# Cosine attention and a gated feed-forward layer: from 112-row tiles in pairs of heads to 128-lane tiles in quads, with every engine's order written by hand

## The chip, the cores and the metric

One core of one Trainium2 chip runs the kernel. The metric is the device time of one execution in microseconds (us), the median over the runs of a kernel. The profile is of one execution; its times are us unless marked ns.

## What is computed

```python
q_n = q / (norm(q, axis=-1) + 1e-06)          # q, k, v: 8 batches, 12 heads, 448 rows, 64 columns, fp32
k_n = k / (norm(k, axis=-1) + 1e-06)
attn = softmax(q_n @ k_n.T / tau)             # tau = 0.1
x = (attn @ v) with the heads side by side    # 3584 x 768
H = max(x @ w_h, 0);  T = sigmoid(x @ w_t + b_t)   # w_h, w_t: 768 x 768
out = T * H + (1 - T) * x                     # 3584 x 768, fp32
```

Both kernels write T as (1 + tanh)/2, so the softmax's denominator carries a factor 2 (the column of 2.0 beside v) and the bias a factor 0.5. Scores are at most 1/tau, so no maximum is subtracted.

## The kernel before

All 448 rows of a head are four chunks of 112 rows, and 112 of the 128 partitions are used. Heads go in six pairs for each batch.

For each pair `emit_A` (L89) loads q and k (L92, 224 KB each, in pieces of 256 bytes), squares them on GpSimd (POOL, L97) and sums the squares on VectorE (DVE, L104). `emit_rsqrt` (L107) turns the sums into reciprocal norms by shifts and two Newton steps of small DVE instructions. `emit_B` (L146) scales q and k on POOL (L152), transposes them with eight TensorE (PE) matmuls against the identity (L157), copies the result out of PSUM on DVE (L164), and loads v and casts it on ScalarE (ACT, L174). `emit_qkt` (L177) gives the scores, transposed: for each pair eight matmuls of 448 columns (L186), two heads on the two halves of the rows of PE; ACT takes the exponential of two score tiles in one instruction of 112x896 (L194). `emit_av` (L201) multiplies by v with the exponentials as weights: 16 matmuls of 65 columns for each head (L208), then a reciprocal (L219) and a multiplication (L220) on DVE.

The feed-forward layer (FFN) takes the rows of a batch in four tiles of 112. For each tile `emit_xt` (L229) transposes six blocks on PE (L234), which DVE copies out (L240); `emit_ffn_quarter` (L242) runs 6 matmuls of 384 columns for a half of x @ w_h (L255, then DVE's L274) and 6 and one for the bias (L263) for a half of x @ w_t (then ACT's tanh, L271); `emit_ffn_final` (L283) combines them on DVE (L291, L299) and stores 336 KB (L307).

The loops at L315 and L330 lay the order of emission: all of batch 0's preparation first, then, head by head, batch b's attention, batch b-1's FFN and batch b+1's preparation. Batch 0 runs without FFN work beside it and the last batch's FFN runs alone at the end. Within this, the order on each engine is chosen by a scheduler from the dependences and priorities (`high_priority`). All loads and stores go through the queue of SyncE (SP).

## Time and profile before

| | |
|---|---|
| time, median of 2 runs (lowest, highest) | 514.92 (513.39, 516.46) |
| span of the profiled execution, first to last instruction | 509.7 |
| what lies around the span in such an execution | 3.7 to 6.8, 5.2 by the median |
| mean granted clock of PE, of 1 | 0.887 |
| instructions | 8460 |
| bytes moved by DMA | 49.31 MB |

The profile is of one execution, and which of the two runs it belongs to is not told; so the time around the span is given as the difference to either. A busy PE in the profile is not PE at its peak, since its matmuls are pipelined; the time that PE really needs is read from the distance between starts in the timeline.

### The profile page before, as it was taken

How to read it: one execution, taken by the hardware profiler on the slowest of the kernel's cores; microseconds unless marked ns; L12 is line 12 of the kernel's file. 1: busy time of each engine (PE TensorE's matmuls, PEld its weight loads, DVE VectorE, ACT ScalarE, POOL GpSimd, SP SyncE). 2: the span in 40 equal slices, each digit the busy share in tenths (PEclk: the TensorE clock that was granted, in tenths of full speed). 3: DMA queues.
4: the chain of work that ended last, by engine and by line, in shares of the span. 5: the costliest groups of instructions: out<-in, count | busy, mean ns of one | idle time of the engine just before them, and what ended most of it. 6: DMA issues, size and time to landing. Idle time of an engine off the chain costs nothing.

```text
span 509.7 us, 8460 instructions
## 1 busy us (share of the span) xinstructions
PE 412.6 (81%) x3328; PEld 286.6 (56%) x3328; DVE 314.3 (62%) x661; ACT 226.1 (44%) x305; POOL 201.7 (40%) x198
## 2 busy tenths in 40 slices
PE   0545945988776979889878999989887999899995
PEld 0114604766554656557655666657564767575774
DVE  3655465458277675666777494938685455453574
ACT  1321441346335453354453473454546455644511
POOL 3663296723924276337170833282517030000000
PEclk9999999999967797677898797959897899797999
DMA  9960695725553157415551554255231221000012
GB/s 173 224 167 1 211 192 105 147 57 129 109 117 81 39 131 140 100 46 113 142 110 45 132 123 103 62 118 138 70 74 46 64 65 46 27 28 28 29 55 81
DMA packets 137033, 49.31 MB, mean 97 GB/s; under 512 B 131873, under 2 KB 131873, under 8 KB 136994
## 3 DMA queue, kind: packets, MB, share of 16 engines
q1 hardware_dynamic: 136994, 48.77, 42.9%
q8 instruction: 26, 0.43, 0.4%
q14 instruction: 13, 0.11, 0.1%
HBM read 37.75 MB, written 11.01 MB: 96 GB/s over the span
## 4 chain that ended last, share of the span: by engine, by line
PE 53%; DVE 23%; ACT 5%; POOL 5%; SPq 5%; DMA 4%; issue 3%; POOLq 0%; ACTq 0%
PE pt L255 24%; PE u L208 15%; PE sT L186 9%; DVE outst L299 6%; DVE th1a L291 6%; DVE n L104 4%; PE qkT L157 4%; POOL qkn L152 3%; ACT expt L194 3%; SPq L92 3%; DMA qk_raw<-in_k_dram 3%; ACT tt L271 2%; DMA qk_raw<-in_q_dram 2%; POOL qk_sq L97 2%; DVE xTb L240 1%
## 5 line engine op out<-in xcount | busy, mean ns | idle before, releaser
L194 ACT ACTIVATE expt<-sT 112x896 f16<-112x896 f32 x192 | 166.7, 916 | 96.5 <-PE sT L186 77.7
L208 PEld LDWEIGHTS <-expt 112*112 112x112 f16 x1536 | 115.5, 158 | 40.1 <-issue 17.4
L208 PE MATMUL u<-vp,expt 112*112 112x65 f16 x1536 | 121.5, 238 | 12.9 <-DVE xbach L220 9.2
L255 PEld LDWEIGHTS <-xTb 128*112 128x112 f16 x768 | 101.8, 145 | 47.8 <-DVE xTb L240 15.0
L152 POOL TENSOR_TENSOR qkn<-qk_raw,yy 112x512 f16<-112x512 f32 x96 | 99.7, 1068 | 72.4 <-DVE yy L144 37.7
L186 PE MATMUL sT<-qkt 64*112 64x448 f16 x384 | 104.3, 437 | 26.3 <-ACT expt L194 25.6
L97 POOL TENSOR_TENSOR qk_sq<-qk_raw 112x1024 f16<-112x1024 f32 x48 | 96.3, 2013 | 29.5 <-DMA qk_raw<-in_k_dram 23.3
L255 PE MATMUL pt<-w_h_f,xTb 128*112 128x384 f16 x384 | 100.0, 402 | 5.4 <-DVE xTb L240 4.4
L174 ACT CAST vp<-v_raw 112x512 f16<-112x512 f32 x48 | 29.8, 621 | 118.8 <-PE u L208 78.8
L255 PE MATMUL pt<-w_t_f,xTb 128*112 128x384 f16 x384 | 77.2, 330 | 0.4 <-DVE hmx L274 0.3
L104 DVE TENSOR_REDUCE n<-qk_sq 112x16 f16<-112x1024 f16 x48 | 58.0, 1211 | 26.2 <-POOL qk_sq L97 26.2
L291 DVE SCALAR_TENSOR_TENSOR th1a<-tt,hmx 112x384 f16<-112x384 f16 x64 | 51.1, 798 | 33.2 <-ACT tt L271 33.2
L157 PE MATMUL qkT<-ident,qkn 112*128 112x112 f16 x384 | 35.5, 247 | 44.2 <-POOL qkn L152 40.9
L186 PEld LDWEIGHTS <-qkt 64*112 64x112 f16 x384 | 31.2, 140 | 62.3 <-issue 55.4
L173 POOL MEMSET vp<- 112x8 f16 x48 | 6.9, 149 | 147.4 <-PE u L208 147.4
L274 DVE SCALAR_TENSOR_TENSOR hmx<-pt,xbach 112x384 f16<-112x384 f32 x64 | 35.2, 553 | 39.2 <-PE pt L255 39.2
L271 ACT ACTIVATE tt<-pt 112x384 f16<-112x384 f32 x64 | 31.4, 491 | 62.6 <-PE pt L263 62.0
L157 PEld LDWEIGHTS <-qkn 112*128 112x128 f16 x384 | 28.5, 116 | 54.5 <-POOL qkn L152 45.7
L219 DVE RECIPROCAL rd<-u 112x4 f32<-112x4 f32 x96 | 17.2, 179 | 55.3 <-PE u L208 54.4
L299 DVE SCALAR_TENSOR_TENSOR outst<-xbach,th1a 112x384 f32<-112x384 f16 x64 | 49.2, 769 | 1.0
L164 DVE COPY qkt<-qkT 128x896 f16<-128x896 f16 x48 | 29.8, 620 | 21.1 <-PE qkT L157 11.8
L220 DVE SCALAR_TENSOR_TENSOR xbach<-u,rd 112x256 f16<-112x256 f32 x96 | 40.3, 421 | 1.9
(55 smaller groups left out, 116.8 us busy)
## 6 DMA issues: line engine op xcount, KB each, us to landing
qk_raw<-in_q_dram SPq DMA_DIRECT2D x48, 224.0 KB, 4.4
qk_raw<-in_k_dram SPq DMA_DIRECT2D x48, 224.0 KB, 4.4
v_raw<-in_v_dram SPq DMA_DIRECT2D x48, 224.0 KB, 3.4
out_dram<-outst SPq DMA_DIRECT2D x32, 336.0 KB, 2.8
w_raw<-in_moe_w_h_dram SPq DMA_DIRECT2D x1, 2304.0 KB, 10.8
w_raw<-in_moe_w_t_dram SPq DMA_DIRECT2D x1, 2304.0 KB, 8.7
bt_raw<-in_moe_b_t_dram SPq DMA_DIRECT2D x1, 3.0 KB
```

Of the source, the lines that this page charges most:

```text
L97: nc.gpsimd.tensor_mul(qk_sq[:P], qk_raw[:P], qk_raw[:P])
L104: nc.vector.reduce_sum(n2[:P, pr], qk_sq[:P], axis=AX.X)
L152: nc.gpsimd.tensor_mul(qkn[:P, t], qk_raw[:P, t], in1)
L157: nc.tensor.transpose(qkT[:, t, c * P : (c + 1) * P], qkn[:P, t, c], ident[:P, :P],)
L186: nc.tensor.matmul(sTs[hh][:P, jj, 0:S], lhsT=qkt[hh * D : (hh + 1) * D, 1, jc * P : (jc + 1) * P], rhs=qkt[hh * D : (hh + 1) * D, 0, 0:S] ...
L194: nc.scalar.activation(st["expt", b, 2 * pr + hh][:P, 2 * g : 2 * g + 2, :], sTs[hh][:P, :, 0:S], AF.Exp, scale=inv_tau,)
L208: nc.tensor.matmul(u[:P, ic, 0 : D + 1], lhsT=expt[:P, jc, ic * P : (ic + 1) * P], rhs=vp[:P, jc, hh], start=(jc == 0), stop=(jc == NC - 1),)
L220: nc.vector.scalar_tensor_tensor(out=xb[:P, pr, :, hh, :], in0=u[:P, :, 0:D], scalar=0.0, in1=rd[:P, :].unsqueeze(2).to_broadcast([P, NC, D]),
L255: nc.tensor.matmul(pt[:P, :], lhsT=xT[:, cc, ic * P : (ic + 1) * P], rhs=w_f[:, cc, mh * MH : (mh + 1) * MH], start=(cc == 0), stop=(cc == ...
L271: nc.scalar.activation(tt[:P, mh], pt[:P, :], AF.Tanh)
L291: nc.vector.scalar_tensor_tensor(out=th1a[:P, mh], in0=tt[:P, mh], scalar=1.0, in1=hmx[:P, mh], op0=ALU.add, op1=ALU.mult,)
L299: nc.vector.scalar_tensor_tensor(out=outst[:P, mh * MH : (mh + 1) * MH], in0=xg, scalar=2.0, in1=th1a[:P, mh], op0=ALU.mult, op1=ALU.add,)
```

## The change

The program is written anew. A quad is four heads (24 quads for 8 batches), a step is one exponential of 128x896 (seven for each quad, 168 in all).

- **Layouts.** Of each head 384 rows are three chunks of 128 on all 128 partitions; the 64 rows left are tails, and the tails of two heads share a chunk (for k and v with zeros in the other head's place). Loads take pieces of 768 bytes for the 384 rows and 256 for the tails. The FFN takes three tiles of 128 rows for each batch, and one tile of 128 rows from the tails of two batches.
- **Transposes of q and k** are two DMA transposes for each quad from SP's queue (L220 of 128x896, L226 of 128x1024, SBUF to SBUF) in place of 16 PE matmuls and two DVE copies for each pair.
- **Engines.** q is squared on ACT (L141), k on POOL (L147); v is cast on DVE (L236, L243); the scaling stays on POOL (L182 to L211), but for q of the first quad.
- **Order.** `manual_schedule` (L68): each engine executes in the order of emission. In step g that is the scores of step g+1, the exponential of g, a part of the products with v, about 4.6 FFN matmuls from a queue (`ffn_run`), then the pieces of preparation that `prep` lists for the step. What is left of the FFN queue runs at the end.

The core of the diff:

```diff
-    def emit_A(b, pr):
-    def emit_rsqrt(b, prs=None):
-    def emit_B(b, pr):
-    def emit_qkt(b, pr, g):
-    def emit_av(b, h):
-    def emit_xt(b, ic):
-    def emit_ffn_quarter(b, ic, qq):
-    def emit_ffn_final(b, ic):
-    def ffn_slot(bprev, h):
...
+    ctx.enter_context(tc.manual_schedule())
...
+    NV = 3
+    kn_b = [const.tile([128, 8, 128], FP16, name=f"kn{i}") for i in range(NV)]
+    vm_b = [const.tile([128, 12, 66], FP16, name=f"vm{i}") for i in range(NV)]
+    vt_b = [const.tile([128, 2, 2, 66], FP16, name=f"vt{i}") for i in range(NV)]
...
+    def load_qk(Q, kq=None):
+        kq = kq or nc.sync
+        b, qd = divmod(Q, NQ)
+        raw = raw_p.tile([128, 28, 64], FP32, name="raw")
+        st["raw", Q] = raw
+        for src, g0, eng in ((q, 0, nc.sync), (k, 14, kq)):
+            hs = src[b, 4 * qd : 4 * qd + 4]
+            eng.dma_start(
+                raw[:, g0 : g0 + 12].rearrange("p (h j) d -> p h (j d)", j=3),
+                hs[:, 0:MAIN].rearrange("h (p j) d -> p h (j d)", j=3),
+            )
+            for i in range(2):
+                if g0 == 0:
+                    t = hs[2 * i : 2 * i + 2, MAIN:S]
+                else:
+                    t = hs[:, MAIN:S].rearrange("(s h) p d -> h s p d", h=2)[i]
+                eng.dma_start(
+                    raw[64 * i : 64 * i + 64, g0 + 12 : g0 + 14],
+                    t.rearrange("h p d -> p h d"),
+                )
...
+    def sq_q(Q):
+        sq = sq_p.tile([128, 14, 64], FP16, name="sqq")
+        st["sqq", Q] = sq
+        nc.scalar.activation(sq[:, :, :], st["raw", Q][:, 0:14, :], AF.Square)
+    def sq_k(Q):
+        sq = sq_p.tile([128, 14, 64], FP16, name="sqk")
+        st["sqk", Q] = sq
+        rk = st["raw", Q][:, 14:28, :]
+        nc.gpsimd.tensor_mul(sq[:, :, :], rk, rk)
...
+    def norm_q(Q, i, eng=None):
+        eng = eng or nc.gpsimd
+        _, rs, _, qd = n2rs(Q)
+        raw = st["raw", Q]
+        if i == 0:
+            st["qn", Q] = qn_p.tile([128, 7, 128], FP16, name="qn")
+        qn = st["qn", Q]
+        if i < 2:
+            eng.tensor_mul(
+                qn[:, 4 * i : 4 * i + 3, :].rearrange("p j (h d) -> p h j d", h=2),
+                raw[:, 6 * i : 6 * i + 6].rearrange("p (h j) d -> p h j d", h=2),
+                rs[:, qd, 6 * i : 6 * i + 6].rearrange("p (h j) -> p h j", h=2)
+                .unsqueeze(3).to_broadcast([128, 2, 3, D]),
+            )
...
+    def turn(Q, t):
+        if t == 0:
+            qT = qt_p.tile([128, 7, 128], FP16, name="qT")
+            nc.sync.dma_start_transpose(
+                qT[:, :, :], st.pop(("qn", Q))[:, :, :].rearrange("p c x -> p (c x)")
+            )
+            st["qT", Q] = qT
+        else:
+            kT = qt_p.tile([128, 8, 128], FP16, name="kT")
+            nc.sync.dma_start_transpose(
+                kT[:, :, :], kn_b[Q % NV][:, :, :].rearrange("p c x -> p (c x)")
+            )
+            st["kT", Q] = kT
+            st.pop(("raw", Q))
...
+    def qk(g):
+        Q, ci = divmod(g, 7)
+        qT = st["qT", Q][:, :, :].rearrange("p c x -> p (c x)")
+        kT = st["kT", Q]
+        sp = s_ps.tile([128, 2, 512], FP32, name="sp")
+        st["sp", g] = sp
+        if ci == 0:
+            for s in range(2):
+                nc.tensor.matmul(
+                    sp[:, s, 0:S], lhsT=kT[:, 6 + s, :], rhs=qT[:, s * S : (s + 1) * S],
+                    start=True, stop=True,
+                )
+        else:
+            s = (ci - 1) // 3
+            for h in range(2):
+                hp = slice(64 * h, 64 * h + 64)
+                nc.tensor.matmul(
+                    sp[:, h, 0:S], lhsT=kT[hp, ci - 1, :], rhs=qT[hp, s * S : (s + 1) * S],
+                    start=True, stop=True,
+                )
...
+        nc.scalar.activation(
+            st["e", Q][:, o : o + 2 * S].rearrange("p (a n) -> p a n", a=2),
+            st.pop(("sp", g))[:, :, 0:S],
+            AF.Exp,
+            scale=inv_tau,
+        )
+    def av_slot(Q, u, slot, s, h, w):
+        e, vm, vt = st["e", Q], vm_b[Q % NV], vt_b[Q % NV]
+        for kc in range(4):
+            if kc < 3:
+                o = (s * 3 + kc) * 2 * S + h * S + w
+                rhs = vm[:, (2 * s + h) * 3 + kc, 0 : D + 1]
+            else:
+                o = 12 * S + s * S + w
+                rhs = vt[:, s, h, 0 : D + 1]
+            nc.tensor.matmul(
+                u[:, slot, :], lhsT=e[:, o : o + 128], rhs=rhs,
+                start=(kc == 0), stop=(kc == 3),
+            )
...
+        for i in range(3 * part, 3 * part + 3):
+            t, h = divmod(i, 2)
+            av_slot(Q, u, i, s, h, (64 if s else 0) + 128 * t)
+        if part == 1:
+            b, qd = divmod(Q, NQ)
+            x, _ = x_tile(b)
+            rd = nrm_p.tile([128, 6], FP32, name="rd")
+            nc.vector.reciprocal(rd[:, :], u[:, :, D])
+            h0 = 4 * qd + 2 * s
+            nc.vector.scalar_tensor_tensor(
+                out=x[:, :, h0 : h0 + 2, :],
...
+    def ffn_items(b, t):
+        xs = st["xtail", b // 2][:, :, :] if t == 3 else st["x", b][:, t]
+        xf = xs.rearrange("p h d -> p (h d)")
+        loc = {}
+        def tr():
+            xp = p_ps.tile([128, CC, 128], FP16, name="xp", tag="pt")
+            for c in range(CC):
+                nc.tensor.transpose(xp[:, c, :], xf[:, c * 128 : (c + 1) * 128], ident[:, :])
+            loc["xT"] = xt_p.tile([128, CC, 128], FP16, name="xT")
+            nc.vector.tensor_copy(loc["xT"][:, :, :], xp[:, :, :])
...
+            def one(cc):
+                def f():
+                    if cc == 0:
+                        first()
+                    nc.tensor.matmul(
+                        loc["pt"][:, :], lhsT=loc["xT"][:, cc, :], rhs=w_f[:, cc, ms],
+                        start=(cc == 0), stop=(cc == CC - 1 and w_i == 0),
+                    )
+                    if cc == CC - 1 and w_i == 0:
+                        nc.vector.scalar_tensor_tensor(
+                            out=loc["hm"][:, ms], in0=loc["pt"][:, :], scalar=0.0,
+                            in1=xf[:, ms], op0=ALU.max, op1=ALU.subtract,
+                        )
+                        fin(ms, mh)
+                return f
+            def bias():
+                nc.tensor.matmul(
+                    loc["pt"][:, :], lhsT=ones_row[:, :], rhs=bth[:, ms],
+                    start=False, stop=True,
+                )
+                nc.scalar.activation(loc["tt"][:, ms], loc["pt"][:, :], AF.Tanh)
...
+        def fin(ms, mh):
+            th = ff_p.tile([128, MH], FP16, name="th")
+            nc.vector.scalar_tensor_tensor(
+                out=th[:, :], in0=loc["tt"][:, ms], scalar=1.0, in1=loc["hm"][:, ms],
+                op0=ALU.add, op1=ALU.mult,
+            )
+            nc.vector.scalar_tensor_tensor(
+                out=loc["o"][:, ms], in0=xf[:, ms], scalar=2.0, in1=th[:, :],
+                op0=ALU.mult, op1=ALU.add,
+            )
...
+    load_qk(0, nc.scalar)
+    load_v(0)
+    load_qk(1)
+    load_qk(2)
+    nc.gpsimd.memset(kn_b[0][:, 6:8, :], 0.0)
...
+    for Q in range(2):
+        sq_q(Q)
+        sq_k(Q)
+        red(Q, 0)
+        red(Q, 1)
+        rsqrt(Q)
+        for i in range(3):
+            norm_q(Q, i, nc.vector if Q == 0 else None)
+        for i in range(4):
+            norm_k(Q, i)
+        turn(Q, 0)
+        turn(Q, 1)
+        for i in range(3):
+            cast_v(Q, i)
+    load_qk(3)
...
+        N = slot + 2
+        own = [R for R in (slot + 2,) if R == 2] + [R for R in (slot + 3,) if 3 <= R < 6]
+        far = [R for R in (slot + 5,) if 6 <= R < NQUAD]
+        at = 0
+        for R in own:
+            put(at, sq_q, R)
+            put(at, sq_k, R)
+            put(at + 1, red, R, 0)
+            put(at + 1, red, R, 1)
+            put(at + 1, rsqrt, R)
+            at += 2
+        for R in far:
+            put(at, sq_q, R)
+            put(2, sq_k, R)
+            put(at + 2, red, R, 0)
+            put(5, red, R, 1)
+            if R % NQ == NQ - 1:
+                put(6, rsqrt, R - 2, 3)
+        if N < NQUAD:
+            o = 2 if N == 2 else 0
+            put(o + 0, norm_q, N, 0)
+            put(o + 1, norm_q, N, 1)
+            put(o + 1, norm_q, N, 2)
+            put(o + 2, norm_k, N, 0)
+            put(o + 3, norm_k, N, 1)
+            put(o + 3, norm_k, N, 2)
+            put(o + 3, norm_k, N, 3)
+            put(o + 2, turn, N, 0)
+            put(o + 4, turn, N, 1)
+            put(4, cast_v, N, 0)
+            put(5, cast_v, N, 1)
+            put(5, cast_v, N, 2)
+        if 6 <= slot + 6 < NQUAD:
+            put(5, load_qk, slot + 6)
+        if slot % NQ == 1 and slot // NQ + 2 < B:
+            put(3, load_v, slot // NQ + 2)
...
+    ffq = []
+    credit = 0.0
+    RATE = 4.6
+    def ffn_run(amount):
+        nonlocal credit
+        credit = min(credit + amount, 9.0)
+        while ffq and credit > 0:
+            c, f = ffq.pop(0)
+            f()
+            credit -= c
...
+    qk(0)
+    L = None
+    for g in range(NSTEP):
+        if g % 7 == 0:
+            L = prep(g // 7)
+        if g + 1 < NSTEP:
+            qk(g + 1)
+        ex(g)
+        av_step(g)
+        ffn_run(RATE)
+        for f, a in L[g % 7]:
+            f(*a)
+    for g in range(NSTEP, NSTEP + 3):
+        av_step(g)
+        ffn_run(RATE)
+    while ffq:
+        ffn_run(9.0)
```

On DVE, in the middle of the program, where one FFN tile ends (`th1a`, `outst` before; `th`, `o` after) and the next begins. Before:

```order
L140 TENSOR_SCALAR tt__1964<-tt__1964 112x96
L104 TENSOR_REDUCE n2_2317<-qk_sq_2315 112x16
L291 SCALAR_TENSOR_TENSOR th1a_1752<-tt_1646,hmx_1647 112x384
L144 TENSOR_TENSOR yy_1962<-yy_1962,tt__1964 112x96
L299 SCALAR_TENSOR_TENSOR outst_1753<-xbach_622,th1a_1752 112x384
L219 RECIPROCAL rd_1782<-u_1765 112x4
```

After:

```order
L321 SCALAR_TENSOR_TENSOR x_3236<-u_3322,rd_3363 128x3x128
L151 TENSOR_REDUCE n2_3374<-sqq_3314 128x14
L386 SCALAR_TENSOR_TENSOR hm_3249<-pt_3370,x_2640 128x384
L407 SCALAR_TENSOR_TENSOR th_3391<-tt_3250,hm_3249 128x384
L411 SCALAR_TENSOR_TENSOR o_3251<-x_2640,th_3391 128x384
L365 COPY xT_3427<-xp_3420 128x768
L236 CAST vm0_114<-vr_2801 128x12x64
```

The scheduler had strewn the pieces of several chains between each other; now the copy that the next tile's matmuls wait for (`xT`) stands behind the reduction and the three last instructions of the tile before, in one fixed row.

On SP, at the start of the program (`qk_raw`, `v_raw`, `raw` are the tiles that loads fill; `qT`, `kT` are transposed). Before:

```order
L92 DMA qk_raw_307<-in_k_dram 112x8x64
L168 DMA v_raw_340<-in_v_dram 112x8x64
L73 DMA w_raw_345<-in_moe_w_h_dram 128x6x768
L79 DMA bt_raw_351<-in_moe_b_t_dram 1x768
L92 DMA qk_raw_359<-in_q_dram 112x8x64
```

After:

```order
L91 DMA raw_139<-in_k_dram 128x4x192
L100 DMA raw_139<-in_k_dram 64x2x64 x2
L220 DMA_TRANSPOSE qT_193<-qn_185 128x7x128
L226 DMA_TRANSPOSE kT_195<-kn0_111 128x8x128
L220 DMA_TRANSPOSE qT_222<-qn_214 128x7x128
L226 DMA_TRANSPOSE kT_224<-kn1_112 128x8x128
L91 DMA raw_229<-in_q_dram 128x4x192
```

The first transposes stand behind the loads of three quads and of batch 0's v, and the loads of the fourth quad behind the transposes of the first two.

## Rows read from the trace of the kernel before

**Rows 1.** Busy time by stretch: start:end, length, each engine's busy us (instructions), PEclk, DMA share, GB/s.

```profile
0.00:62.00 62.00, 28.98 (x179) 17.10 (x180) 32.80 (x95) 18.15 (x23) 26.31 (x32) 1.00 0.67 152
62.00:460.00 398.00, 342.21 (x2844) 239.33 (x2843) 255.28 (x510) 191.78 (x259) 175.36 (x167) 0.87 0.43 94
460.00:510.00 50.00, 41.38 (x310) 30.14 (x307) 26.20 (x57) 16.14 (x25) 0.00 (x0) 0.91 0.16 49
```

**Rows 2.** The chain that ended last, shares of the span by engine.

```profile
PE 53%; DVE 23%; ACT 5%; POOL 5%; SPq 5%; DMA 4%; issue 3%; POOLq 0%; ACTq 0%
```

**Rows 3.** Who waited for whom: us in total, times, longest.

```profile
PE qkT L157 <- POOL qkn L152: 40.9, 11, 15.5
...
PEld L255 <- DVE xTb L240: 15.0, 23, 1.7
```

**Rows 4.** Timeline, PE in three stretches: start, length to the last end, what, xcount.

```profile
202.77 0.56 PE L157 MATMUL qkT<-ident,qkn 112*128 112x112 f16 x8
203.26 0.39 PE L186 MATMUL sT<-qkt 64*112 64x448 f16 x1
204.43 1.02 PE L208 MATMUL u<-vp,expt 112*112 112x65 f16 x16 [0.78 <-DVE xbach L220]
205.38 0.58 PE L186 MATMUL sT<-qkt 64*112 64x448 f16 x3
...
495.10 2.16 PE L255 MATMUL pt<-w_h_f,xTb 128*112 128x384 f16 x12 [0.60 <-DVE xTb L240]
...
499.37 2.11 PE L255 MATMUL pt<-w_h_f,xTb 128*112 128x384 f16 x12
```

**Rows 5.** Groups by line, shapes kept apart: out<-in, xcount, busy us, mean ns, idle before.

```profile
L152 POOL TENSOR_TENSOR qkn<-qk_raw,yy 112x512 f16<-112x512 f32 x96 | 99.7, 1068 | 72.4 <-DVE yy L144 37.7 <-PE qkT L157 31.0 <-DMA qk_raw<-in_q_dram 3.6
L97 POOL TENSOR_TENSOR qk_sq<-qk_raw 112x1024 f16<-112x1024 f32 x48 | 96.3, 2013 | 29.5 <-DMA qk_raw<-in_k_dram 23.3 <-DVE outst L299 2.7 <-DVE th1a L291 1.9
L104 DVE TENSOR_REDUCE n<-qk_sq 112x16 f16<-112x1024 f16 x48 | 58.0, 1211 | 26.2 <-POOL qk_sq L97 26.2
L291 DVE SCALAR_TENSOR_TENSOR th1a<-tt,hmx 112x384 f16<-112x384 f16 x64 | 51.1, 798 | 33.2 <-ACT tt L271 33.2
L299 DVE SCALAR_TENSOR_TENSOR outst<-xbach,th1a 112x384 f32<-112x384 f16 x64 | 49.2, 769 | 1.0
L220 DVE SCALAR_TENSOR_TENSOR xbach<-u,rd 112x256 f16<-112x256 f32 x96 | 40.3, 421 | 1.9
L274 DVE SCALAR_TENSOR_TENSOR hmx<-pt,xbach 112x384 f16<-112x384 f32 x64 | 35.2, 553 | 39.2 <-PE pt L255 39.2
L271 ACT ACTIVATE tt<-pt 112x384 f16<-112x384 f32 x64 | 31.4, 491 | 62.6 <-PE pt L263 62.0 <-DVE xbach L220 0.5 <-DVE yy L144 0.2
L219 DVE RECIPROCAL rd<-u 112x4 f32<-112x4 f32 x96 | 17.2, 179 | 55.3 <-PE u L208 54.4
L240 DVE COPY xTb<-xTp 128x672 f16<-128x672 f16 x32 | 15.9, 503 | 9.5 <-PE xTp L234 9.5
L76 DVE CAST w_h_f<-w_raw 128x4608 f16<-128x4608 f32 x1 | 2.6, 2551 | 0.0
L144 DVE TENSOR_TENSOR yy<-yy,tt__610 112x96 f32<-112x96 f32 x2 | 0.5, 259 | 0.1
```

**Rows 6.** The same for DVE alone from 420 to 510 us, where POOL is all but idle.

```profile
L291 DVE SCALAR_TENSOR_TENSOR th1a<-tt,hmx 112x384 f16<-112x384 f16 x20 | 11.2, 558 | 15.6 <-ACT tt L271 15.6
L299 DVE SCALAR_TENSOR_TENSOR outst<-xbach,th1a 112x384 f32<-112x384 f16 x20 | 11.1, 553 | 0.5
```

**Rows 7.** DMA issues by line: xcount, KB each, median us to landing.

```profile
qk_raw<-in_q_dram SPq DMA_DIRECT2D x48, 224.0 KB, 4.4
...
w_raw<-in_moe_w_h_dram SPq DMA_DIRECT2D x1, 2304.0 KB, 10.8
```

**Rows 8.** Timeline at the start: SP's last load of batch 0 and the first exponentials.

```profile
18.84 1.26 SPq L168 DMA_DIRECT2D v_raw<-in_v_dram  x1
...
20.85 1.72 ACT L194 ACTIVATE expt<-sT 112x896 f16<-112x896 f32 x2 [6.46 <-PE sT L186]
```

More of the change, by code (lines that the diff above doesn't have):

```diff
@@ new lines @@
+    st = {}
+    def load_qk(Q, kq=None):
[18 more added lines that the diff above has]
+                )
@@ L201, in emit_av @@
-    def emit_av(b, h):
-        pr, hh = h // 2, h % 2
-        vp = st["vp", b, pr]
-        expt = st["expt", b, h]
-        u = pb1_p.tile([128, NC, 128], FP32, name="u", tag="pb1")
-        for ic in range(NC):
-            for jc in range(NC):
-                nc.tensor.matmul(
-                    u[:P, ic, 0 : D + 1],
-                    lhsT=expt[:P, jc, ic * P : (ic + 1) * P],
-                    rhs=vp[:P, jc, hh],
-                    start=(jc == 0),
-                    stop=(jc == NC - 1),
-                )
-        xb = st["xb", b]
-        with tc.high_priority(offset=300):
-            rd = nrm_p.tile([128, NC], FP32, name="rd")
-            nc.vector.reciprocal(rd[:P, :], u[:P, :, D])
+            nc.vector.scalar_tensor_tensor(
+                out=a, in0=y, scalar=-0.5, in1=x, op0=ALU.mult, op1=ALU.mult
+            )
@@ new lines @@
+    load_qk(0, nc.scalar)
[3 more added lines that the diff above has]
+    nc.gpsimd.memset(kn_b[0][:, 6:8, :], 0.0)
+    make_identity(nc, ident)
+    for i in range(NV):
+        if i:
+            nc.vector.memset(kn_b[i][:, 6:8, :], 0.0)
+        nc.vector.memset(vm_b[i][:, :, D : D + 1], 2.0)
+        nc.vector.memset(vt_b[i][:, :, :, :], 0.0)
+        for h in range(2):
+            nc.vector.memset(vt_b[i][64 * h : 64 * h + 64, :, h, D : D + 1], 2.0)
+    nc.vector.memset(bth[:, :], 0.0)
@@ new lines, with prep, put @@
+    nc.vector.tensor_single_scalar(bth[:1, :], bt_raw[:1, :], 0.5, ALU.mult)
+    for i in range(3):
+        load_w(i)
+    load_qk(5)
+    def prep(slot):
+        L = [[] for _ in range(7)]
+        def put(step, f, *a):
+            L[step].append((f, a))
+        N = slot + 2
[34 more added lines that the diff above has]
+            put(3, load_v, slot // NQ + 2)
+        if slot < 3:
+            for s_, i in ((0, 0), (1, 1), (2, 2), (3, 3)):
+                j = slot * 4 + i
+                put(s_ + 3, cast_w, j)
+                if j + 3 < 2 * CC:
+                    put(s_ + 3, load_w, j + 3)
+        return L
@@ new lines, with av_step @@
+    ffq = []
[8 more added lines that the diff above has]
+            credit -= c
+    def av_step(g):
+        Q, ci = divmod(g, 7)
+        if ci == 4 and Q < NQUAD:
+            av_main(Q, 0, 0)
+        elif ci == 5 and Q < NQUAD:
+            av_main(Q, 0, 1)
+        elif ci == 6 and Q < NQUAD:
+            av_tail(Q, 0)
+        elif ci == 0 and Q:
+            av_tail(Q - 1, 1)
+        elif ci == 1 and Q:
+            av_main(Q - 1, 1, 0)
+        elif ci == 2 and Q:
+            av_main(Q - 1, 1, 1)
+            b, qd = divmod(Q - 1, NQ)
+            if qd == NQ - 1:
+                for t in range(3):
+                    ffq.extend(ffn_items(b, t))
+                if b % 2:
+                    ffq.extend(ffn_items(b, 3))
```

406 lines of the change are left out of this document (170 added, 236 removed).

## The prediction

> **What bounds the kernel now.** I first cut the span into stages and read the busy times of each [rows 1]. There are three: 62 us in which batch 0 goes through attention with no feed-forward (FFN) work beside it, 398 us in which seven batches are carried (56.9 us for each), and 50 us of FFN at the end. In the middle stage PE looks 86% busy (342.21 of 398), but matmuls are pipelined, so I priced its work by the distance between starts [rows 4]: 16 products with v from 204.43 to 205.38 are 0.059 us each; eight transposes from 202.77 to 203.26 are 0.061; one score matmul lasts 0.39 and three last 0.58, so a further pair on the two row halves costs 0.19; and 26 FFN matmuls, which are one tile, lie between 495.10 and 499.37: 4.27 us, 0.164 each. A batch of the middle stage thus needs 192 x 0.059 + 104 x 0.164 + 24 x 0.19 + 72 x 0.061 = 37.3 us of PE at full clock. The granted clock there is 0.87 [rows 1], which makes 42.9 of the 56.9 us: PE is filled to 75%, and the rest is waiting. The chain of what ended last says the same: PE 53%, DVE 23%, and the rest in pieces [rows 2]. The largest wait of PE is for POOL's scaled q and k, then there is one for DVE's copy of the transposed x [rows 3]. DVE has 255 of 398 us, ACT 192, POOL 175 [rows 1]. So this is a kernel of several half-full engines that wait for each other, with PE nearest to its bound.
>
> **The change, part by part.** A batch is now 21 steps.
>
> PE. The products with v stay 192 for each batch (64 for a quad, three quads); the weights grow from 112 to 128 columns, so one costs between 0.059, if the columns don't count, and 0.067 in proportion; with 0.063 that is 12.1 us. Scores: 18 pairs on two row halves at 0.19, and three tail pairs that use all rows and so can't run beside each other, 0.38: 4.6 us. FFN: 3.5 tiles in place of 4, each still 26 matmuls: 3.5 x 4.27 = 14.9. Transposes: 21 in place of 72, 1.3 us. Together 32.9 us at full clock, 37.8 at 0.87. So PE saves only 4.4 us of work for each batch; the waits are what can be won.
>
> DVE, for each batch, from rows 5. Six reductions of 896 elements, 896/1024 of 1.211 = 1.06: 6.4. Eight small instructions for the norms at about 0.24 (0.259 on a two-input one): 1.9. Three casts of v of 768 elements (2.551 us for 4608 gives 0.43) with two tails at about 0.17: 2.3; this work comes from ACT. Softmax division: per quad two times 0.18 + 0.55 (the 384-element one from PSUM, as L274) and once 0.18 + 0.42: 6.2. FFN: 3.5 tiles of one copy (0.503 x 768/672 = 0.57) and two times 0.553 + 0.798 + 0.769: 16.8. Together 33.6 us, where before it had 255/7 = 36.5 (a little of that for batch 0). L291 and L299 take 0.558 and 0.553 us where POOL is idle [rows 6] and 0.798 and 0.769 on average [rows 5]; with the low prices DVE has 30.5. I keep the average, since POOL stays at work: k's square 1.76 (896/1024 of 2.013) and 1920 elements of scaling at 1.068/512 make 5.8 us for a quad, 17.3 for a batch.
>
> ACT: 21 exponentials and three squares of q, at 0.86 (two in 1.72 [rows 8]), and seven tanh at 0.491 [rows 5]: 24.1 us. It isn't the bound.
>
> So a batch has floors of 37.8 (PE at the clock of before), 32.9 (PE at full clock), 33.6 (DVE) and 24.1 (ACT). The bounds of what the middle stage costs are 34 us for each batch, if the engines never wait for each other, and 37.8/0.75 = 50, if PE is filled no better than now. Which it is depends on the written order: an instruction that waits holds all behind it on its engine. Speaking for a good fill, scores are issued a step ahead of their exponential and the products a step behind, so PE and ACT have a step's slack. Speaking against, each FFN tile starts with six transposes whose copy on DVE stands behind the last three instructions of the tile before and often behind a reduction: 0.55 + 0.80 + 0.77 + 1.06 + 0.57 = 3.7 us, while PE has some 1.3 us of other work (scores 0.19, 12 products 0.74, six transposes 0.37). A wait of 1 to 2 us, 3.5 times for each batch, is 3.5 to 7 us that nothing hides; the wait for this copy was 15.0 us in all before [rows 3]. PE at full clock with the longer wait gives 39.9, at 0.87 with the shorter one 41.3; I take 40 us. Steps 23 to 167 have FFN work beside them, 145 steps or 6.9 batches: 276 us (235 to 345).
>
> The start. The first exponential came at 20.85, and SP had issued batch 0's 18 loads of 224 KB by 20.1 [rows 8]. Now the loads of three quads and of v stand ahead of the first transposes on SP: 3 x 896 + 1344 = 4032 KB, the same 18 x 224. If bytes set the pace, the transposes issue at 20. A DMA transpose isn't in this trace. The nearest row is a load of about the same size, 4.4 us; the other end is the slowest DMA here, 10.8 us for ten times the bytes [rows 7]. I take 4.4: first exponential at 25. Larger pieces may bring it to 18, the dearer transpose to 32.
>
> Steps 0 to 22 without FFN: 23 x 0.86, and seven squares of q that ACT does between them, 6.0: 25.8. The fourth quad's load is queued behind the transposes of quads 0 and 1, which wait for their scaling on POOL, and ACT's square of it holds the exponentials behind it: I put 4 us for that. 30 us (26 to 34).
>
> The end. 784 units of FFN (28 tiles of 26 matmuls and 2) less 145 x 4.6 leave 117 units, 4.2 tiles. A tile is 4.27 and 0.37 of transposes and some 0.6 of waiting for the copy (0.60 at 495.10 [rows 4]): 22 us. Then the last combination and store: the last tile began its second half at 499.37 and the span ended at 509.7, of which 26 matmuls took 4.3: 5.8. 28 us.
>
> Later transposes are issued nine to eleven steps ahead of their use, some 17 us, so 4.4 us of each lies beside other work; if they cost more than that slack, the third rival decides. The loads get fewer pieces, and the DMA engines had a share of 0.43 in the middle stage [rows 1]: no cost.
>
> The sum: 25 + 30 + 276 + 28 = 359 us of span, where the profiled execution had 509.7. With the 5.2 that separate its span from the median of the runs, 364. Against 514.92 that is 29% less.
>
> Two rules of the Trainium skill bear on this, and the sum does without both. The page "VectorE: DVE Perf Modes" (The three transpose paths) gives 1309 ns for a 128x128 block by DMA; by that price a quad's 15 blocks, one after another, take 19.6 us, 24 quads 471, and the time would be about 530, slower. The page "Advanced Engine Details and Errata" (X-Bar Transpose) says that such transposes are as fast as ordinary DMAs, by which the sum stands. The trace of before has no such transfer. The page "TensorE: Matmul & The Clock Gate" (Weight-path perf modes) says that weights of 128 columns load in a faster way; by it the products with v, whose weights grow to 128 columns, would cost less than they did. The transposes of before already load 128 columns, and at 0.061 us they go no faster than the products with 112 [rows 4], so I give this nothing.
>
> **Rivals.** First, the written order fits and the clock stays up: DVE's 33.6 becomes the bound at 34 us for a batch. For it: PE's work comes in even portions; against: the copy at each tile's start. 25 + 28 + 235 + 25 + 5 = 318.
>
> Second, the waits of the scheduler's version come back as waits in line: 50 us for a batch. For it: DVE's row mixes reductions that wait for POOL with the copies PE waits for; against: squares and scaling are done a quad or more ahead. 25 + 32 + 345 + 28 + 5 = 435, still faster.
>
> Third, the DMA transposes become the bound. They replace 384 PE matmuls that were cheap, and they run through one queue. At 10.8 us each, the dear end [rows 7], a quad takes 21.6 us and 24 quads 518; with the start, the end and what lies around them 25 + 518 + 28 + 5 = 576: slower. It decides as soon as one transpose holds the queue for over 6.7 us, half of a quad's 13.3 us at my pace. Against it: a load of the same bytes lands in 4.4.
>
> **Chances.** My forecast 0.5, the first rival 0.2, the second 0.22, the third 0.06, anything near no change 0.02. The range takes the forecast and most of the two rivals on either side: 315 to 430. About 2% is what a measurement tells from no change here. Faster by over 2%: 0.92; within 2%: 0.02; slower: 0.06.
>
> **What would show it.** Right: windows of the middle stage with PE, at its own busy share, above 90% and DVE above 80%, some 13 us between the first score matmuls of two quads, a first exponential near 25, a transpose landing in under 6 us, and 26 to 30 us after the last exponential. If SP's queue shows transposes back to back and PE waits for kT, the third rival is true. If L365's copy heads PE's waits with over 60 us, it's the second. If the products with v come under 0.045 us apart, the PE term was too dear. A time above 430 or below 315 makes the prediction wrong.

## The result and the profile after

The changed kernel takes 465.68 us (463.36 to 467.99, two runs) against 514.92. The ratio is 0.903, with a 95% interval from 0.8895 to 0.9166: faster, but by a tenth and not by the 29% forecast, and above the range that the prediction gave. The profiled execution has a span of 466.2 us. Runs over 1.5% above the fastest of their kernel count as slow: ratios and intervals leave them out, and of the kernel with both waits removed, below, three runs of four are such, the profiled one among them.

First the busy times by stretch, in the columns of [rows 1]; the stretches are the start, the steps without FFN work beside them, the middle stage, and the end.

```profile
0.00:25.00 25.00, 3.09 (x10) 0.57 (x11) 16.24 (x46) 6.55 (x7) 10.49 (x17) 1.00 0.73 185
25.00:95.00 70.00, 20.05 (x220) 12.05 (x219) 41.28 (x82) 22.87 (x27) 30.57 (x35) 0.88 0.86 218
95.00:428.00 333.00, 248.44 (x2369) 130.55 (x2367) 198.23 (x424) 155.95 (x207) 115.15 (x146) 0.85 0.48 118
428.00:467.00 39.00, 23.92 (x171) 14.18 (x171) 19.85 (x38) 4.46 (x10) 0.00 (x0) 0.92 0.14 51
```

No engine is full anywhere, though the DMA engines have a share of 0.86 in the second stretch. In the middle stage PE has 75% (248.44 of 333), DVE 60%, ACT 47%, POOL 35%. The chain of what ended last, which answers to [rows 2], has lost PE's majority; SP's own instructions and DMA transfers together now make 17% of it, where they made 9%:

```profile
PE 37%; DVE 32%; SPq 9%; DMA 8%; POOL 5%; ACT 4%; issue 4%; DVEq 0%; ACTq 0%; POOLq 0%
```

The waits, which answer to [rows 3] (engine and line, what it waited for: us in all, times, longest):

```profile
PE pt L381 <- DVE xT L365: 66.2, 28, 5.1
ACT sqq L141 <- DMA raw<-in_q_dram: 65.8, 12, 15.5
PE sp L266 <- ACT e L279: 58.2, 20, 9.9
ACT tt L398 <- PE pt L394: 144.4, 53, 7.4
```

POOL's scaling no longer holds PE, as the change meant. In its place stand two waits of nearly the same size. PE waits for the copy of the transposed x at every one of the 28 FFN tiles, 2.4 us on average, where before it was 15.0 us in all (by the row of the weight loads, which is 71.1 us now). And ACT waits for a load of q before it can square it, with the exponentials queued behind the square; much of PE's 58.2 us for the exponentials is the same wait seen one engine further (with the load issued earlier, below, it falls to 15.4). ACT's longest wait is another: its tanh waits 144.4 us for the FFN matmuls of its tile, with exponentials behind it too. It falls with the wait for the copy (to 96.1 us where only that one is removed), so part of it goes with that wait; no run moved the tanh, and what the rest costs is not shown. The same view for SP's queue shows where the load is held up:

```profile
SPq L419 <- DVE o L411: 136.7, 18, 11.6
```

SP stands in line for FFN results to store, and queued behind a store are the transposes and the loads.

How these hang together is seen in the chain, here from 190 to 227 us (start, length, what):

```profile
202.15 0.56 DVE o L411
202.71 0.48 DVE xT L365
203.19 0.10 SPq L425
...
204.02 1.32 SPq L226
...
205.43 0.58 SPq L91
...
206.07 1.26 SPq L100
...
207.38 3.29 DMA raw<-in_q_dram
...
210.74 0.95 ACT sqq L141
211.69 0.81 ACT e L279
...
212.54 0.56 PE sp L266 x2
213.10 0.78 PE u L295 x12
213.88 1.28 PE pt L381 x4
...
217.97 1.07 DVE o L411
219.04 0.48 DVE xT L365
```

Read it as a circle. DVE finishes an FFN tile and copies the next x; SP can store the tile, and behind the store come a transpose and the load of q; the load lands; ACT squares it and can go on with exponentials; the scores, products and FFN matmuls follow; and DVE finishes the next tile, 15.8 us after the last (202.15 to 217.97). From the end of the copy at 203.19 to the square at 210.74 nothing is computed on this circle: 7.5 us of stores, issues and a transfer.

In the steps without FFN work ACT waits for the same square. Its timeline (start, length, what, and in brackets the idle time before it):

```profile
32.96 0.95 ACT L141 ACTIVATE sqq<-raw 128x896 f16<-128x896 f32 x1 [8.59 <-DMA raw<-in_q_dram]
...
44.53 0.95 ACT L141 ACTIVATE sqq<-raw 128x896 f16<-128x896 f32 x1 [5.47 <-DMA vtr<-in_v_dram]
...
62.61 0.95 ACT L141 ACTIVATE sqq<-raw 128x896 f16<-128x896 f32 x1 [15.52 <-DMA raw<-in_q_dram]
...
79.72 0.95 ACT L141 ACTIVATE sqq<-raw 128x896 f16<-128x896 f32 x1 [8.49 <-DMA raw<-in_q_dram]
...
92.77 0.95 ACT L141 ACTIVATE sqq<-raw 128x896 f16<-128x896 f32 x1 [6.90 <-DMA raw<-in_q_dram]
```

The five waits add up to 45.0 us (the second is put down to a load of v). That is as much as this stage is longer than forecast; the runs below show that taking them away gives back less than half of it.

### The profile page after: what moved, and what is told of

Read it like the earlier page. It is cut to its first block, busy times and chain, and to the rows that moved or that the text cites. A ratio compares the mean times of both kernels' runs of the same rounds, so it can differ in the third digit from the quotient of the medians.

```text
span 466.2 us, 7225 instructions
## 1 busy us (share of the span) xinstructions
PE 295.5 (63%) x2768; PEld 157.3 (34%) x2768; DVE 275.6 (59%) x589; ACT 189.8 (41%) x249; POOL 156.2 (34%) x196
## 4 chain that ended last, share of the span: by engine, by line
PE 37%; DVE 32%; SPq 9%; DMA 8%; POOL 5%; ACT 4%; issue 4%; DVEq 0%; ACTq 0%; POOLq 0%
PE pt L381 21%; PE u L295 7%; PE sp L266 6%; DVE o L411 6%; DMA raw<-in_q_dram 6%; DVE th L407 5%; DVE hm L386 4%; DVE n L151 4%; SPq L100 3%; DVE xT L365 3%; DVE x L321 3%; SPq L226 2%; ACT sqq L141 2%; ACT e L279 2%; PE pt L394 2%
## 5 line engine op out<-in xcount | busy, mean ns | idle before, releaser
L279 ACT ACTIVATE e<-sp 128x896 f16<-128x896 f32 x168 | 146.1, 917 | 45.3 <-PE sp L266 30.1
L381 PE MATMUL pt<-w_t_f,xT 128*128 128x384 f16 x336 | 86.2, 376 | 66.2 <-DVE xT L365 66.2
L266 PE MATMUL sp<-qT,kT 64*128 64x448 f16 x288 | 61.8, 424 | 58.4 <-ACT e L279 58.2
L381 PEld LDWEIGHTS <-xT 128*128 128x128 f16 x672 | 61.8, 106 | 108.9 <-DVE xT L365 71.1
L398 ACT ACTIVATE tt<-pt 128x384 f16<-128x384 f32 x56 | 27.5, 491 | 144.4 <-PE pt L394 144.4
L147 POOL TENSOR_TENSOR sqk<-raw 128x896 f16<-128x896 f32 x24 | 41.7, 1737 | 133.1 <-DMA raw<-in_k_dram 114.4
L295 PEld LDWEIGHTS <-e 128*128 128x128 f16 x1536 | 66.5, 106 | 53.3 <-issue 49.1
L381 PE MATMUL pt<-w_h_f,xT 128*128 128x384 f16 x336 | 80.3, 354 | 0.0
L182 POOL TENSOR_TENSOR qn<-raw,rs 128x384 f16<-128x384 f32 x46 | 41.0, 911 | 81.0 <-DVE rs L170 41.8
L295 PE MATMUL u<-vm,e 128*128 128x65 f16 x864 | 56.8, 209 | 17.2 <-DVE x L321 17.2
L141 ACT ACTIVATE sqq<-raw 128x896 f16<-128x896 f32 x24 | 22.8, 948 | 73.4 <-DMA raw<-in_q_dram 65.8
L295 PE MATMUL u<-vt,e 128*128 128x65 f16 x288 | 48.8, 207 | 0.0
L202 POOL TENSOR_TENSOR kn<-raw,rs 128x384 f16<-128x384 f32 x48 | 42.7, 910 | 4.7 <-DVE rs L170 4.7
L151 DVE TENSOR_REDUCE n<-sqq 128x14 f32<-128x896 f16 x24 | 25.8, 1075 | 5.7 <-ACT sqq L141 5.6
L151 DVE TENSOR_REDUCE n<-sqk 128x14 f32<-128x896 f16 x24 | 25.8, 1075 | 0.0
```

Of the source, the lines that this page charges most:

```text
L147: nc.gpsimd.tensor_mul(sq[:, :, :], rk, rk)
L151: nc.vector.reduce_sum(n2[:, qd, 14 * t : 14 * t + 14], st.pop((("sqq", "sqk")[t], Q))[:, :, :], axis=AX.X)
L182: eng.tensor_mul(qn[:, 4 * i : 4 * i + 3, :].rearrange("p j (h d) -> p h j d", h=2), raw[:, 6 * i : 6 * i + 6].rearrange("p (h j) d -> p h ...
L202: eng.tensor_mul(kn[:, 3 * i : 3 * i + 3, :].rearrange("p j (h d) -> p h j d", h=2), raw[:, g : g + 6].rearrange("p (h j) d -> p h j d", h=2),
L266: nc.tensor.matmul(sp[:, h, 0:S], lhsT=kT[hp, ci - 1, :], rhs=qT[hp, s * S : (s + 1) * S], start=True, stop=True,)
L279: nc.scalar.activation(st["e", Q][:, o : o + 2 * S].rearrange("p (a n) -> p a n", a=2), st.pop(("sp", g))[:, :, 0:S], AF.Exp, scale=inv_tau,)
```

## The experiments

Twelve kernels were run, each beside the kernel before on the same chip; ratios are to that. Differences in us from the changed kernel are between medians of different chips, on which the kernel before took 510.3 to 515.5 us. Two kinds of theory stood against each other. One: the written order makes engines wait in line in two places, for the load of q and for the copy of x. The other: the work itself, or the bytes, set the pace, and a wait that is taken away only moves.

**Each wait alone.** First the load, which the changed kernel issues at step 5 of a slot for a square that stands at step 0 of the next:

```
-            put(5, load_qk, slot + 6)
+            put(0, load_qk, slot + 6)
```

> The changed kernel, but each quad's loads of q and k are issued at step 0 of the list (5 steps earlier) instead of step 5, so that seven steps, not two, lie between a load and ACT's square of q. Theory 1 (late loads hold ACT's squares, the squares hold the exponentials behind them in the written order, and PE starves): most of ACT's 72.5 us of waiting for q goes, the middle stage falls from 48 to some 43 us a batch, and the time to 410 to 435. Rival (the wait only shifts to the next thing in line, the copy of xT or the DMA bandwidth): 455 or more.

Measured: 448.2 us, ratio 0.8766 (0.8684 to 0.8848), between the two. Then the copy: the next tile's six transposes and its copy are placed ahead of the last group of matmuls of the tile before.

```
-        return [(2.0, tr)] + mm(1, 0) + mm(0, 0) + mm(1, 1) + mm(0, 1)
+        return [(2.0, tr)], mm(1, 0) + mm(0, 0) + mm(1, 1), mm(0, 1)
...
+                for i, (_, body, end) in enumerate(ts):
+                    ffq.extend(body)
+                    if i + 1 < len(ts):
+                        ffq.extend(ts[i + 1][0])
+                    ffq.extend(end)
```

> The changed kernel, but within a batch the six transposes of the next FFN tile and their copy on DVE are put ahead of the last group of matmuls of the tile before, so the copy stands ahead of that group's three DVE instructions. Theory 2 (the copy in line at each tile's start is a wait of PE that nothing hides): PE's 66 us of waiting for xT falls below 25, and the time falls by 25 to 50 us, to 415 to 440. Rival (PE isn't what ends last, so its wait is replaced by a wait for the exponentials): 455 or more.

Measured: 446.07 us, ratio 0.8728 (0.864 to 0.8816), 6 us above the theory's range. Each edit did to its wait what it should, but the other wait grew. First the waits with the early load, then those with the transposes ahead:

```profile
PE pt L381 <- DVE xT L365: 74.0, 28, 5.1
ACT sqq L141 <- DMA raw<-in_q_dram: 19.2, 4, 8.5
```

```profile
ACT sqq L141 <- DMA raw<-in_q_dram: 98.8, 16, 15.7
PE pt L381 <- DVE xT L365: 17.9, 12, 2.4
```

With the copy's wait gone PE and DVE come sooner to the place where ACT waits, and the load is no sooner there: 33 us of the 48 that PE no longer waits for the copy come back as ACT's wait for q.

**Both together.**

> Both edits of the first runs together: the loads of a quad issued at step 0 of a slot and the next tile's transposes ahead of the last FFN group of the tile before. Alone they gave 17.5 and 19.6 us. Theory (two separate waits in line, ACT for q's load and PE for the copy of the transposed x): they add up, 425 to 433 us, with the wait of the FFN matmuls for the copy under 25 us and ACT's for q under 30 us. Rival (one wait only hides the other; what one edit frees the other finds taken): 440 to 448.

Measured: 388.78 us (one run of 381.37, three from 388.47 to 389.66; the quotient of the medians is 0.762, without an interval). Both expectations fell, on the good side: alone the edits had given 17.5 and 19.6 us, together 76.9. By the ratios that is 2.9%, 3.3% and 16% of the changed kernel's time. The waits, in the same view:

```profile
ACT sqq L141 <- DMA raw<-in_q_dram: 21.0, 5, 8.6
PE pt L381 <- DVE xT L365: 18.8, 13, 2.4
```

Read by stage (from the first exponential to the first copy of an FFN tile, and from there to the end of the last exponential), the two waits account for most of it in the middle stage. All are us:

| kernel | steps 0 to 22 | middle stage | wait for q in it | wait for the copy in it |
|---|---|---|---|---|
| changed | 76.1 | 330.9 | 22.7 | 58.2 |
| early load | 71.1 | 312.8 | 0 | 65.9 |
| transposes ahead | 75.9 | 313.7 | 55.5 | 16.0 |
| both | 71.9 | 261.3 | 1.9 | 16.8 |

The middle stage falls by 18, 17 and 70 us where the sum of its two waits falls by 15, 9 and 62. The steps 0 to 22 fall by 5 us at most.

**Distance or place.** The load moved in the runs above also changed its place among SP's stores and transposes. So, with the transposes ahead and every load where the changed kernel has it, q's square was moved instead:

```
-            put(at, sq_q, R)
+            put(3, sq_q, R)
...
-            put(at + 2, red, R, 0)
+            put(5, red, R, 0)
```

> The transposes ahead, as in the first runs, and q's square three steps later (step 3 of a slot in place of 0, its sum at step 5), with every load where the changed kernel has it. Theory (ACT's square stands in line too soon behind its load, and this wait and the one for the copy each hide the other): moving the square does what moving the load did, 380 to 400 us, with ACT's wait for q under 30 us. Rival (what helped was the place of the load among the stores and transposes on SP, not its distance to the square): 425 to 446, near the 446.07 of the transposes ahead alone.

Measured: 403.58 us, ratio 0.7807 (0.7742 to 0.7871), 4 us above the theory's range and 21 below the rival's. ACT's wait for q is 37.0 us, in place of the 98.8, where under 30 was expected. So most of the gain comes from the distance between a load and the instruction that stands in line for it, and either end of it may be moved.

**SP's own order.** A tile's store is held back until the middle of the next tile:

```
-            if mh == 1:
+            if mh == 0:
+                flush()
+            else:
+                held.append(put_out)
```

> Only the store of an FFN tile's output is moved: it is issued half a tile later, when its result is long there. In the changed kernel SP stands in line 136.7 us for results to be stored, and the loads and transposes of q and k are queued behind those stores. Theory (SP's order is what makes the loads late): 445 to 455 us, SP's wait for the output under 30 us, and ACT's wait for q down from 65.8 to under 30. Rival (SP is idle anyway and the loads are late because they are issued only two steps ahead of the square): 460 to 468 with ACT's wait unchanged.

Measured: 449.54 us, ratio 0.8794 (0.8726 to 0.8861). The time is the theory's, the waits are not: SP's wait for the output only falls to 65.0 us, since half a tile isn't always enough, and ACT's for q to 52.0. Of these, 45.3 lie ahead of the first FFN tile, where no output is stored; in the middle stage ACT's wait falls from 22.7 to 6.7 us and the stage from 330.9 to 314.0. In place of the results, SP now stands in line for POOL's scaled k ahead of the transposes (56.4 us by the line L226, before 25.9). That loads stand behind stores is a part of their lateness, worth some 16 us.

**The start.** The loads of quads 3 and 4 go ahead of the transposes of quad 1 on SP:

```
+        if Q == 1:
+            load_qk(3)
+            load_qk(4)
         sq_q(Q)
...
-    load_qk(3)
-    load_qk(4)
     load_v(1)
```

> Only the loads of quads 3 and 4 are moved: they stand on SP behind the transposes of quad 0 and ahead of those of quad 1, where they were behind those of quad 1. Theory (the stage without FFN is long because SP's order makes these loads late): the first exponential of quad 2 comes at 55 to 62 us in place of 67.8, and the time falls to 455 to 461. Rival (the bytes set the pace: 15 MB go through the DMA queues from 25 to 100 us at over 190 GB/s): quad 2 starts within 3 us of 67.8 and the time is 463 to 468.

Measured: 461.8 us, ratio 0.9017 (0.8953 to 0.9081). Quad 2 starts its exponentials at 61.5 in place of 67.8, as the theory said, but quad 5 starts at 117.8 in place of 122.6, the time is just above the theory's range, and the ratio doesn't tell it from the changed kernel's 0.903. A second try at the start, the cast of the bias (which holds DVE idle for 18.9 us until 42.95, waiting for 3 KB of bias that SP issues at 39.89) put off to the fourth quad, gave nothing:

> The changed kernel, but the one small DVE instruction that halves the bias is issued at the start of the fourth quad, not ahead of the third quad's reductions. Theory 3 (it holds all of DVE for 18.9 us while its 3 KB wait behind 3 MB of loads, and PE waits 17.2 us for DVE's division): 445 to 455. Rival (the loads behind it would have held ACT and DVE anyway): 460 to 467.

Measured: 462.66 us, ratio 0.9078 (0.8992 to 0.9164). Quad 2 starts at 63.6 us in place of 67.8, and 3 us are left at the end, within the noise.

**All together**, with q's square at step 3 too:

> All together: early loads, transposes ahead, late stores, loads of quads 3 and 4 ahead of the transposes of quad 1, the cast of the bias later, and q's square at step 3 of its slot in place of 0 (so ten steps behind its load, not two). Theory (the middle stage is lengthened by waits in line and by nothing else that is large): ACT's wait for q under 10 us, the copy's under 25, and 400 to 420 us. Rival (with the waits gone DVE or the granted clock holds it at 43 us and more for a batch): 425 to 435.

Measured: 380.33 us, ratio 0.7451 (0.7394 to 0.7508). It beats both ranges. ACT's wait for q is 4.4 us and the copy's 17.4, as the theory said. The first copy of an FFN tile starts at 79.10 us (97.11 in the changed kernel), so 18 us are gained ahead of the middle stage. The middle stage itself takes 268.4 us, not less than the 261.3 with two edits, and the lowest run of that kernel, 381.37, is level with this one: beyond both waits the further edits give nothing that is clear of the noise. Two windows of the middle stage:

```profile
150.00:200.00 50.00, 41.21 (x438) 21.98 (x436) 42.35 (x84) 29.00 (x39) 25.34 (x29) 0.95 0.89 198
200.00:250.00 50.00, 41.68 (x430) 22.06 (x429) 42.28 (x84) 29.39 (x39) 20.56 (x24) 0.91 0.69 161
```

DVE has 85% of them, PE 83% (which overstates PE, since its matmuls are pipelined), ACT 58%. Two runs were to test whether DVE is the bound. More FFN work in a step (5.2 units in place of 4.6):

> The kernel with all edits together, and 5.2 units of FFN work in a step where it had 4.6. 145 steps then take 754 of the 784 units, and the end has 30 left in place of 117. Theory (the stage with FFN work is held by DVE, so more work in a step only moves time from the end into it): within 2% of 380.33 us. Rival (the middle stage has room): the end shrinks from 32 to some 14 us and the time is 364 to 371.

Measured: 387.39 us, ratio 0.7535 (0.7489 to 0.7582), 1.1% above the kernel it was made from. But the edit hardly moved any work: 96 of the 672 FFN matmuls on w_h and w_t come after the last exponential, where it was 108, and the time from there to the end only falls from 31.1 to 28.3 us. The last batch's four tiles (96 matmuls) can't begin before its products with v are done, which the expectation's 30 units left out. So this run says nothing on whether the stage has room. Less work for DVE does:

```
-            nc.vector.tensor_copy(
+            nc.scalar.copy(
                 vm_b[Q % NV][:, :, 0:D],
```

(and the same for the two tails of v):

> The kernel with all edits together, and the casts of v (43.3 us of DVE's 292.2) done by ACT. Theory (with the waits gone DVE is what holds the middle stage): 352 to 368 us. Rival (ACT's exponentials wait behind the casts, or PE holds it): 374 to 390.

Measured: 360.81 us, ratio 0.7037 (0.6982 to 0.7092). All of the gain lies in the middle stage (268.4 to 248.5 us), so DVE's work held that stage, and this version beats both kernels, by 30% and 22%. The same edit in the changed kernel, with its waits in place, is the counter-test:

> The changed kernel with only the casts of v done by ACT; with all other edits made this was worth 19.5 us. Theory (the waits in line hold the changed kernel, and DVE's amount of work becomes the bound only when they are gone): 458 to 472 us, no gain beyond 2%. Rival (DVE's work is a part of the pace in any case, since its copy of the transposed x comes sooner): 440 to 452.

Measured: 463.75 us, ratio 0.9029 (0.8953 to 0.9104), the ratio of the changed kernel. Busy time by engine, first with the waits gone, then with them:

```profile
PE 269.7 (75%) x2768; PEld 147.6 (41%) x2768; DVE 262.9 (73%) x517; ACT 221.2 (62%) x321; POOL 163.1 (45%) x196
```

```profile
PE 293.7 (64%) x2768; PEld 157.1 (34%) x2768; DVE 244.9 (53%) x517; ACT 220.3 (48%) x321; POOL 152.8 (33%) x196
```

In the second DVE lost 30.7 us of its 275.6 and nothing came of it. The work of an engine is worth something only where it isn't waiting in line.

**A price by itself.** The prediction gave nothing for the wider weights of the products with v. In the kernel before, the products for three of the four chunks of rows got 128 columns of weights in place of 112, and nothing else was changed (the 16 columns more belong to the next chunk, and what they add isn't used):

```
+                w = 128 if ic < NC - 1 else P
                 nc.tensor.matmul(
-                    u[:P, ic, 0 : D + 1],
-                    lhsT=expt[:P, jc, ic * P : (ic + 1) * P],
+                    u[:w, ic, 0 : D + 1],
+                    lhsT=expt[:P, jc, ic * P : ic * P + w],
```

> The kernel before, but three of four products with v take weights of 128 columns, not 112 (16 columns of the next block, whose results nobody reads). Theory 4 (a load of 128 columns is quicker than one of 112, and this alone makes the products of the changed kernel 0.032 us apart): the wide ones stand 0.03 to 0.035 us apart beside narrow ones at 0.05 to 0.06 in the same run, and the time falls by up to 4%. Rival (what made them quicker is the full 128 rows or the new layout): wide ones at 0.06 or more, and the time stays.

Measured: 484.67 us, ratio 0.9502 (0.9423 to 0.9582). Its weight loads, by shape (count | busy us, mean ns):

```profile
L209 PEld LDWEIGHTS <-expt 112*128 112x128 f16 x1152 | 55.0, 108 | 45.1 <-issue 20.6 <-DVE xbach L221 13.3 <-ACT expt L194 3.1
L209 PEld LDWEIGHTS <-expt 112*112 112x112 f16 x384 | 32.7, 153 | 0.2
```

More columns, and 108 ns in place of 153. The products come as the theory said: by the median over the trace, wide ones start 0.033 us apart and narrow ones 0.052 (0.052 in the kernel before, 0.033 in the changed one). The gain is 5.0%, a little more than its 4%; the mean granted clock went from 0.887 to 0.914 with it, and the two weren't told apart.

## Why the prediction was wrong

Set against the sum of 25 + 30 + 276 + 28, the profiled execution has 21.0 us to the first exponential, 76.1 from there to the first copy of an FFN tile (97.11), 330.9 to the end of the last exponential (428.04), and 38.2 after it; around the span lie 1.8 us, where 5.2 were added. The start was near (448 KB of quad 0's k come through ACT's queue and not SP's, and the first transposes issue at 15.4 and 16.9, not at 20); two terms carry the error, 46 and 55 us.

**The step that failed** in the middle stage is one half-sentence, put against the second rival: "squares and scaling are done a quad or more ahead". They are ahead of their use, by nearly five quads. But they stand only two steps behind the issue of their load, and on ACT, in front of exponentials that are due at once. I measured the distance from the square to whoever needs it, and not from the load to the square, so this wait was put at nothing; it is 22.7 us in that stage. The wait for the copy of x was there, at 1 to 2 us for each tile; it is 2.4 (66.2/28), a little small. Neither is the cause by itself: with either one removed the middle stage stays at 313 us, and part of what one edit frees comes back as the other wait. With the distance made longer and the copy moved, it falls to 261.3 us (93.0 to 354.3), 37.9 for each of its 6.9 batches, where I had forecast 40.

That this comes near 40 is in part luck. PE's term in it was 6 us too dear (below); with the measured price the same sum gives some 34 for a batch. And what holds the stage once the waits are gone is DVE's work, shown for the kernel with all edits: the engine that the first rival names, and not PE with a wait beside it.

**Steps 0 to 22** failed at another step. They were priced by ACT alone, 25.8 us, and 4 for the wait of the fourth quad's square. ACT's five waits for squares, 45.0 us, are about the excess of 46, but cutting them doesn't give it back: the early load cuts them to 21.0 us and the stage still takes 71.1; with all edits 0.6 is left, and it takes 58.2. So 18 of the 46 us went with the edits, and 28 stayed with these waits gone. Here is the stage with all edits, and then with the casts of v taken from DVE too:

```profile
20.85:79.10 58.25, 26.48 (x246) 14.77 (x244) 47.02 (x93) 25.93 (x30) 36.64 (x42) 1.00 1.07 270
```

```profile
20.85:79.33 58.48, 26.50 (x246) 14.78 (x245) 38.50 (x75) 29.86 (x39) 36.08 (x42) 1.00 1.06 267
```

ACT's 25.9 us are close to the forecast's 25.8; DVE alone has 47.0 us of work there, which the term left out. With 8.5 us of that work gone the stage is no shorter, while the DMA engines stay at 1.07 and 1.06. So the bytes are the likeliest bound, but no run took bytes away, and this cause stays open.

**The loads** were costed at nothing because "the DMA engines had a share of 0.43 in the middle stage". That looked at one stage and at the engines. In the steps 0 to 22 the share is 0.79, and in the middle stage (0.48 now) it is the queue that counts: the loads are late in part because SP stands in line for a result to store, and the late stores bear that out with some 16 us.

**PE's term** was too dear, which the prediction named as a possible finding: under 0.045 us for a product with v. Twelve of them lie between these two rows of the changed kernel, 0.38 us or 0.032 each:

```profile
203.80 0.27 PE L295 MATMUL u<-vm,e 128*128 128x65 f16 x3
...
204.18 0.97 PE L381 MATMUL pt<-w_t_f,xT 128*128 128x384 f16 x5
```

So they take 6.1 us for a batch in place of 12.1, and PE's floor was 26.9 us at full clock, not 32.9. The rule of the Trainium skill on 128 columns of weights ("TensorE: Matmul & The Clock Gate", Weight-path perf modes) holds here: weight loads of 128 columns took 108 ns beside 153 for 112. I had set it aside because the transposes of before, with 128 columns, were no faster [rows 4]; but 112 columns stream through in a transpose and 65 in such a product, so that was no comparison of weights. The profile of before had one, in the weight loads of the products and of the transposes (x count | busy us, mean ns):

```profile
L208 PEld LDWEIGHTS <-expt 112*112 112x112 f16 x1536 | 115.5, 158 | 40.1 <-issue 17.4
L157 PEld LDWEIGHTS <-qkn 112*128 112x128 f16 x384 | 28.5, 116 | 54.5 <-POOL qkn L152 45.7
```

The error made the forecast longer, and so nearer to the time measured.

**DVE and ACT** were sized well. With both waits gone, DVE has 210.77 us from 90 to 353 us, 30.5 for a batch (28.7 in the changed kernel, 198.23/6.9), where 33.6 was forecast with contention from POOL and 30.5 without. ACT's forecast was 24.1; in the changed kernel it is 22.6 (155.95/6.9).

**The end** was forecast at 28 us and took 38.2. It has the wait for the copy at each tile too, 1.96 us at 433.73, where 0.6 was forecast. With all edits it is some 31. (The prediction reads 499.37 as the start of the last tile's second half; all 26 matmuls of that tile follow it [rows 4], and the rest is 6.0 us, not 5.8.)

**The rivals.** The second one came true, by the very test given for it: the copy heads PE's waits with over 60 us (66.2), and a batch takes 48 us (330.9/6.9), where it said 50. Its 435 us fell short by 44 us in the steps 0 to 22 and 10 at the end, and gave 21 too many to the start, the middle stage and what lies around the span. The first didn't come: 48 us and not 34 for a batch, and some 39 even with all edits. The third fell. The transposes land in 3.2 and 3.3 us (line, count, median us to landing):

```profile
qT<-qn SPq DMA_TRANSPOSE x24, 3.3
kT<-kn SPq DMA_TRANSPOSE x24, 3.2
```

That is no longer than the 4.1 us of a load. It agrees with the Trainium skill's page "Advanced Engine Details and Errata" (X-Bar Transpose). The Trainium skill's 1309 ns for one block ("VectorE: DVE Perf Modes", The three transpose paths) can't be multiplied by the blocks of a transpose: an estimate by it would be 9.2 us for the seven blocks of qT, which land in 3.3.

What stays open besides the start: whether ACT's tanh, in line ahead of exponentials, costs anything of its own.

## What to carry to other kernels

In an order written by hand, list for each instruction that waits for a transfer what stands behind it on its engine, and count the distance from the issue of the transfer (with all that its queue must wait for ahead of it) to that instruction, not from there to the use. Where the waits found lie on one circle through several engines, price them together: each of two edits alone gave 3 to 4%, both some 16% of the changed kernel's time. Price a stage by every engine and by its transfers, and don't take a wait of the right length for its cause: in the steps 0 to 22 the waits went and most of the time stayed. And ask which engine is the fullest only after that: the same casts taken from DVE were worth 2 us, within the noise, with the waits in place, and 19.5 us without.

## What the runs showed of the hardware that was not expected

A weight load of 128 columns took 108 ns where one of 112 took 153, in one kernel, and 16 more columns of weights in three quarters of the products with v made the kernel before 5% faster. SP is held for 1.28 us, by the median, by the issue of one DMA transpose (1.32 at 204.02; 1.22 at the least, 3.73 at the most), so two transposes and the 4.5 us of a quad's six loads (205.43 to 209.97) make 7 us of SP's time in each quad, over half of the 12.0 us that a quad takes in the fastest version ((317.8 - 89.0)/19 between the first exponentials of quads 4 and 23). The mean granted clock was no higher with one wait gone (0.855 and 0.839 in the profiled runs, 0.870 and 0.854 in the two of the changed kernel), but 0.886 with both gone, 0.956 with all edits and 0.974 in the fastest version; PE's busy time fell from 295.5 to 269.7 us for the same matmuls.
